# Reordering the hand-over from attention to a GLU block: unit order, an earlier projection, one early weight read, paced reads, later copies and sums

## The chip, the cores and the metric

The kernel runs on one core of one Trainium2 chip. The core has five engines that run their own instruction lists in order and meet only at semaphores: TensorE (PE, with its weight loads PEld), VectorE (DVE), ScalarE (ACT), GpSimd (POOL) and SyncE (SP). SP, ACT and POOL also issue the DMA transfers. The metric is device time in microseconds (us) of one execution; the time before is the median of three runs. The profile is one execution recorded by the hardware profiler; all its times count from the start of its span.

## The reference

The input is x with 2048 rows and 576 columns, in float32. The output is a transformer block:

```python
q, k, v = qkv[0], qkv[1], qkv[2]                 # 32 heads of 18 columns
off = jnp.arange(W) * dil                        # W = 8, dil = 2: rows s, s-2, ..., s-14
idx = pos[:, None] - off[None, :]
...
logits = jnp.einsum("bhsd,bhswd->bhsw", q, kg) * scale
logits = jnp.where(mask[None, None, :, :], logits, -1e9)
attn = _softmax(logits, axis=-1)
o = jnp.einsum("bhsw,bhswd->bhsd", attn, vg)
...
h = x + _A_ref(_layernorm(x, axis=-1), A_wqkv, A_wo)       # attention, projection by wo
g = jnp.einsum("bsd,df->bsf", x, w_gate)                   # F = 4608
u = jnp.einsum("bsd,df->bsf", x, w_up)
h = _sigmoid(g) * u
...
h2 = h + _B_ref(_layernorm(h, axis=-1), B_w_gate, B_w_up, B_w_down)
```

## The kernel before

**Blocks and precision.** The 2048 rows are four blocks of 512: block b stands for even or odd rows (attention looks back in steps of two, so these never mix) and for the first or the second half of them. Every large matrix product is done with operands split into a high and a low part (`split`, line 103: a copy on ACT, a subtraction on DVE) and three matmuls for each pair of parts.

**First stage: QKV, attention, projection of block 0.** `qkv(b, g, ...)` (line 354) is one call: block b, group g of eight heads, four passes of 14 matmuls, one `yield` after each pass, and stores of q, k and v to scratch memory. `attention(at, b, g, o)` (line 159) is one unit for the same pair: it reads q, k and v back on SP and computes the window of eight positions almost entirely on DVE, in 16 steps that end in a `yield`. For block 0 the result stays on the chip in `o`; for the others it is written to scratch by a DMA on POOL (the spill, line 209). `att_all` (line 375) lists the units in the order (0,0), (0,1), (1,0), (1,1), (0,2), (0,3), (1,2), (1,3), and `step(ag, n)` advances that list by n steps between passes of `qkv`. The calls follow their own order; the last ones are (1,2), (0,3), (2,2), (3,2), (1,3), (2,3), (3,3). `front` (line 445) is the projection of block 0: for four tiles of rows it transposes `o`, multiplies by wo, adds x, normalises and transposes again (`proj_j`, line 228), and makes the first GLU operands `X["a00"]` and `X["a01"]`. Lines 471 to 484 set it in place: calls (1,3) and (2,3), then what is missing of unit (0,3), then two rounds of the projection placed behind the last pass, then call (3,3) with one round after each pass, then the rest.

**Second stage: the GLU.** `items` (line 911) is a list of 86 pieces of 128 hidden columns each: 14 "std" for block 0 alone, 22 "pair" for blocks 0 and 1, 14 std for block 1 (operands `X["a10"]` and `X["a11"]`), then 36 pairs for blocks 2 and 3. The variable `c` counts them. An std item is 28 matmuls of 512 columns plus its share of the down projection; a pair item uses seven products in place of eight and runs from operand sums (`s1` to `s4`) of two blocks. The weights of item c + 2 are read into `wg` (`load_gu`, line 502, two buffers) when item c begins, and those of item c + 1 are split (`weights`, line 510). The first two reads go out on POOL (lines 915, 916) into a pool of tiles that is opened when the first stage's pools are closed.

**Work beside the items.** While PE runs items, a second list `bg` is advanced by `bg_step`, eight steps in an std item and up to seven in a pair. `under_first` (line 830) holds what is left of the attention of block 1, then, not before item 5, its projection `proj_scr` (line 751) and the operand sums for the first pairs; `finish_bg` ends it when item 14 begins. `under_rest` (line 847) does the same for blocks 2 and 3. `proj_scr` reads the spilled attention (tiles `oj`), x (tiles `hj`) and the split wo (tile `wow`) through `load_j` (line 745) and line 793 on SP: four `oj` reads with two steps each, then the others during the first two rounds.

**Down projection and the end.** Sums over items are added in DRAM by accumulating DMAs on POOL: `add_dram` (line 667) into `hacc` for blocks 0 and 1, which copies the finished block to the output right after the last addition, and `down_seven` (line 707) into `hsev` for blocks 2 and 3. `seven` (line 996) forms hidden sums in the pool `dk`, which is opened inside item 50 (line 1085) over memory that stage tiles held until then. `load_tails` (line 1016) reads `hsev` back near the end, adds three pieces on DVE at once (line 1029), and waits ten steps; the last down products are added to these tiles and stored.

**The order on each engine** is made when the kernel is built, from the order of the program and its priorities: `tc.high_priority` moves instructions forward among those that are ready, and `tc.issue_after(ins)` keeps the instructions it covers behind `ins` on the same engine's list without any wait of their own.

Of the kernel before, what the change touches and what calls it, by code (L numbers as in the profile page):

```python
# [15 lines left out]
F32 = mybir.dt.float32  # L16
# [44 lines left out]
def kernel(ctx, tc, x, wqkv, wo, wmlp, out):  # L61
# [36 lines left out]
    def f32(ap):  # L98
        return ap.bitcast(F32)
# [274 lines left out]

    def att_all():
        nonlocal o
        for b, g in ((0, 0), (0, 1), (1, 0), (1, 1), (0, 2), (0, 3), (1, 2), (1, 3)):
            while (b, g) not in emitted:
                yield
            if o is None:  # L380
                o = tok_tile()
            yield from attention(at, b, g, None if b else o[:, :, g * CG:(g + 1) * CG])
            if (b, g) == (0, 3):
                for j in range(NS):
                    dve.tensor_copy(o[:, j, D:DX], o[:, j, DM:D])
                ready.append(b)
# [81 lines left out]

    X = {}
    fr = front()  # L470
    for b, g in ((1, 3), (2, 3)):
        for _ in qkv(b, g, T[b], w[g]):
            step(ag, 1 if ready else 4)
    while not ready:
        step(ag, 1)
    last = passes[-1]
    with tc.issue_after(getattr(last, "ins", last)):
        for _ in range(2):
            next(fr)
    for _ in qkv(3, 3, T[3], w[3]):  # L480
        next(fr, END)
        step(ag, 1)
    with tc.high_priority(HI):
        drain(fr)
    ps_stk.close()
# [15 lines left out]

    def load_gu(f, eng=sp, n=WC):
        ws = gw.tile([P, WC], F32, bufs=2, name="wg")
        eng.dma_start(ws[:, :n], wmlp[f][:, :n])
        return ws

    def d_tile():
        return gd.tile([P, 2, D], F32R, bufs=4, name="d")
# [129 lines left out]
        between(6)  # L638

    tails = {}  # L640
    segs = [0] * 2

    def down_tile(seg, t, j):
        js = slice(j * P, (j + 1) * P)
# [21 lines left out]

    def add_dram(b, hs):
        pool.dma_start(hacc[b], hs, accum_op=ALU.add, max_dma_last_dim=8 * D)
        segs[b] += 1
        if segs[b] == 1 + (NF - NSTD) // 2:  # L670
            e, hf = BLOCKS[b]
            pool.dma_start(ov[e, hf], hacc[b])

    def down_units(seg, b):
        hs = st.tile([P, NS, D], F32, name="stage")
# [69 lines left out]
    def load_j(pj, b, j, i):  # L745
        e, hf = BLOCKS[b]
        t = pj.tile([P, D if i else DX], F32, bufs=NS, name="hj" if i else "oj")
        sp.dma_start(t, (xv[e, hf] if i else oscr[b])[:, j])
        return t

    def proj_scr(pj, b, raw, wos, ins=None, after=None):
        e, hf = BLOCKS[b]
        th, tl = th_tile(), tl_tile()

        def tile_j(t, j):
            js = slice(j * P, (j + 1) * P)
            xj = []

            def put(pv, cs):
                if cs.start == 0:  # L760
                    if b < 2:
                        pool.dma_start(hacc[b][:, j], t[1])
                    else:
                        rows = slice(0, 7, 6) if b == 2 else slice(2, 5, 2)
                        pool.dma_start(hsev[:, j // 2, rows, j % 2],
                                       t[1].rearrange("p (i n) -> p i n", i=2))
                    if raw is None:
                        xj.append(pj.tile([P, 5, P], F32, bufs=2, name="xj"))
                act.activation(xj[0][:, cs] if raw is None else raw[:, cs, js], pv, AF.Copy)

            yield from proj_j(bg_bank, t, wos, th[:, :, js], tl[:, :, js], lambda: t[0], put, (1, 0))
            if raw is None:
                act.dma_start(xscr[b][:, :, js], xj[0])

        todo = []
        if ins is None:
            ins = []
            for j in range(NS):
                ins.append([load_j(pj, b, j, 0), None])
                yield  # L780
                yield
            todo = [0, 1, None, 2, 3]
        live = [tile_j(t, j) for j, t in enumerate(ins)]
        n = 0
        for _ in range(5):
            for gn in live:
                if todo and n % 2 == 0:
                    j = todo.pop(0)
                    if j is not None:
                        ins[j][1] = load_j(pj, b, j, 1)  # L790
                    elif wos[0] is None:
                        ww = pj.tile([P, 2, 5, DH2], F32R, name="wow")
                        sp.dma_start(f32(ww), wscr[0])
                        wos[0] = ww[:, 0], ww[:, 1]
                n += 1
                next(gn)
                yield
        nxt = []
        for j, gn in enumerate(live):
            yield from gn  # L800
            if after is not None:
                nxt.append([load_j(pj, after, j, i) for i in range(2)])
        if raw is not None:
            act.dma_start(xscr[b][:, 0:2], raw[:, 0:2])
        return nxt
# [106 lines left out]
             + [("std", 1, f) for f in range(NSTD)] + [("pair", 1, f) for f in range(NF)])  # L912
    bg = under_first()
    with tc.high_priority(2 * HI):
        wg = load_gu(0, pool)
        wg2 = load_gu(1, pool)
        wc = weights("std", wg, True)
    wg = wg2
# [97 lines left out]
    def load_tails():  # L1016
        nonlocal st
        dk_stk.close()
        st_stk.close()
        st = st_stk.enter_context(sb_pool("st3"))  # L1020
        dz = ctx.enter_context(sb_pool("dz", "right"))
        for b, rows in ((2, ((0, 1), (6, None))), (3, ((2, 5), (4, 3)))):
            hs = tails[b] = st.tile([P, 2, 2, 2 * DH2], F32, name=f"tail{b}")
            for h, (k, k2) in enumerate(rows):
                sp.dma_start(hs[:, h], hsev[:, :, k].rearrange("p u i n -> p u (i n)"))
                if k2 is not None:
                    h2 = dz.tile([P, 2, 2 * DH2], F32, name=f"more{b}{h}")
                    sp.dma_start(h2, hsev[:, :, k2].rearrange("p u i n -> p u (i n)"))
                    dve.tensor_tensor(hs[:, h], hs[:, h], h2, ALU.add)
        yield from lag(10)  # L1030

    def twice(i):
        bg_step(i)
# [2 lines left out]

    for c, (kind, p, f) in enumerate(items):
        w, d = wc
        skip = () if kind == "std" else (3,)
        by_seven = c >= NF + NSTD  # L1040
        if c == NSTD:
            finish_bg()
            last_x = splits[-1]
            bg = under_rest(getattr(last_x, "ins", last_x))
        if c == NF + NSTD:
            finish_bg()
            with tc.high_priority(HI):
                for n in ("s1", "a11"):
                    Xn[n] = x_half(*raw[n])
            X = Xn  # L1050
            pp_stk.close()
            dw = ctx.enter_context(sb_pool("dw", "right"))
        if c + 1 < len(items):
            wc = weights(items[c + 1][0], wg, c + 1 < NF + NSTD)
        if c + 2 < len(items):
            wg = load_gu(items[c + 2][2], n=WC if c + 2 < NF + NSTD else GU)
        hid = {}
        blocks = [p] if kind == "std" else [2 * p, 2 * p + 1]

        def last(h0, h1):  # L1060
            hid[0] = hidden(*h0, "h0")
            hid[1] = hidden(*h1, "h1")

        if kind == "std":
            hid = single(X, w, p, late, twice)
        elif not by_seven:
            side = last_pair if c == NF - 1 else bg_step

            def between(i):
                if i in (4, 6):  # L1070
                    units(2)
                side(i)

            pair(X, w, between, last)
        else:
            def between(i):
                nonlocal st, gc, gc_bufs, dk
                units(1)
                if c == NF + NSTD and i == 5:
                    assert not queue  # L1080
                    st_stk.close()
                    gc_stk.close()
                    gc = gc_stk.enter_context(sb_pool("gc2"))
                    st = st_stk.enter_context(sb_pool("st2"))
                    dk = dk_stk.enter_context(sb_pool("dk", "right"))
                    gc_bufs = 2
                down_side(f, i)

            pair(X, w, between, last if f >= NF - NPL else last_sums(f))
            if f < NF - NPL:  # L1090
                if f % 2:
                    if f == 1:
                        queue.append(lag(LAG))
                    queue.append(seven())
                continue
            d = M[f]
        seg.append((hid, d))
        if len(seg) == 2:
            if by_seven and f == NF - NPL + 1:
                queue.append(load_tails())  # L1100
            for b in blocks:
                queue.append(down_std(seg, b, f // 2) if kind == "std" else
                             down_tail(seg, b, f == NF - 1) if by_seven else down_units(seg, b))
            seg = []
# [44 lines left out]
```

## Time and profile before

| | |
|---|---|
| median of 3 runs | 1642.64 us (1641.17 to 1648.43) |
| the profiled execution, its own time | 1647.17 us |
| its span in the profile | 1645.4 us |
| mean granted TensorE clock | 0.979 |
| PE, DVE, ACT, POOL busy | 96%, 78%, 53%, 11% |
| stages of the span, roughly | QKV and attention to 206 us, first items from 251, pairs from 416, second std items from 807, pairs of blocks 2 and 3 from about 1010 to 1616 us, last sums to the end |

The page gives busy shares of every engine and a chain of waits that is followed back from the last instruction. A row of the timeline reads: start, length (both us), engine, line, operation, output and inputs by the program's names, shapes, number of merged instructions, and in brackets how long the engine was idle before it and what ended that time. A row of the chain reads: start, length, what. A row of stretches gives for each engine the busy time and the number of instructions, then the granted clock, the DMA share and GB/s.

### The profile page before, as it was taken

What the parts mean: (1) busy time and instruction counts of PE and PEld (TensorE: products, weight loads), DVE (VectorE), ACT (ScalarE), POOL (GpSimd) and SP (SyncE); (2) the same over time, 40 slices, a digit from 0 to 9 for tenths busy, and PEclk for the clock granted to TensorE, in tenths of its full rate; (3) what the DMA queues carried; (4) which work ended last, traced back from release to release, by engine and by line L of the source; (5) the groups of instructions that cost most, each with busy time, mean ns of one, the idle gap of its engine ahead of it and who ended that gap; (6) DMA issues with size and microseconds to landing.
All of it is one profiled execution on the core that took longest, in us unless ns stands there. A gap on an engine that the chain in (4) does not pass through costs nothing.

```text
span 1645.4 us, 22460 instructions
## 1 busy us (share of the span) xinstructions
PE 1573.6 (96%) x8532; PEld 1392.6 (85%) x8532; DVE 1279.6 (78%) x2002; ACT 873.6 (53%) x1535; POOL 185.2 (11%) x228
## 2 busy tenths in 40 slices
PE   7899887999999999999979999999999999999998
PEld 6799775898888888888968987888888888888887
DVE  7999999558999999999626677777767777677755
ACT  5422224325556566656424344677667776677651
POOL 2000010010000100100111100121121211212210
PEclk9999987999999999999989999999999999999999
DMA  7446635525366666575856335598888888988882
GB/s 252 164 160 230 223 123 186 180 90 190 106 180 154 178 148 175 150 192 142 247 141 215 120 129 147 109 190 174 172 176 163 189 175 172 178 169 177 184 185 91
DMA packets 79613, 276.66 MB, mean 168 GB/s; under 512 B 8368, under 2 KB 16816, under 8 KB 78480
## 3 DMA queue, kind: packets, MB, share of 16 engines
q0 software_dynamic: 28144, 108.74, 34.1%
q1 hardware_dynamic: 40160, 142.75, 27.0%
q10 hardware_dynamic: 11200, 23.73, 3.8%
q8 instruction: 67, 1.10, 0.3%
q14 instruction: 42, 0.34, 0.1%
HBM read 147.19 MB, written 130.35 MB: 169 GB/s over the span
## 4 chain that ended last, share of the span: by engine, by line
PE 62%; issue 15%; DVE 10%; DMA 6%; POOL 4%; ACT 2%; SPq 0%; POOLq 0%; DVEq 0%; ACTq 0%
PE b L544 31%; PE dp L652 14%; PE b L551 6%; PE dp L718 6%; POOL h L727 3%; DMA wg<-in_wmlp_dram 3%; PE acc L150 2%; DVE pr L198 2%; DVE pr L172 1%; DVE lg L175 1%; PE b L150 1%; PE bgp L150 1%; DVE pr L203 1%; DMA h<-stage 1%; DVE pr L205 1%
## 5 line engine op out<-in xcount | busy, mean ns | idle before, releaser
L544 PE MATMUL b<-tl,w 128*128 128x512 f32 x1728 | 447.3, 399 | 18.4 <-DVE w L105 7.6
L544 PEld LDWEIGHTS b<-tl,w 128*128 128x128 f32 x1728 | 315.6, 190 | 80.2 <-DVE w L105 8.3
L544 PE MATMUL b<-th,w 128*128 128x512 f32 x1380 | 359.3, 395 | 0.0
L544 PEld LDWEIGHTS b<-th,w 128*128 128x128 f32 x1380 | 251.9, 189 | 53.7 <-DVE s L626 4.0
L551 PE MATMUL b<-th,w 128*128 128x512 f32 x576 | 178.2, 391 | 0.0
L104 ACT ACTIVATE w<-wg 128x384 fp32r<-128x384 f32 (+2 forms) x200 | 118.1, 596 | 108.7 <-DMA wg<-in_wmlp_dram 45.1
L105 DVE TENSOR_TENSOR w<-wg,w 128x384 fp32r<-128x384 f32 (+2 forms) x200 | 128.5, 648 | 52.6 <-ACT w L104 52.5
L724 ACT ACTIVATE ev<-dp 128x576 f32<-128x576 f32 x224 | 144.8, 647 | 32.9 <-PE dp L718 30.2
L727 POOL DMA_DIRECT2D h<-ev x128 | 109.7, 857 | 461.4 <-ACT ev L724 454.0
L150 PE MATMUL acc<-qw,th 128*128 128x432 f32 x512 | 155.6, 364 | 0.0
L105 DVE TENSOR_TENSOR w<-tw,w 128x512 fp32r<-128x512 f32 x116 | 79.5, 686 | 72.3 <-ACT w L104 71.7
L551 PEld LDWEIGHTS b<-th,w 128*128 128x128 f32 x576 | 108.7, 189 | 23.2
L652 PE MATMUL dp<-d,h0h 128*128 128x288 f32 x640 | 120.6, 298 | 0.0
L652 PE MATMUL dp<-d,h1h 128*128 128x288 f32 x640 | 120.2, 297 | 0.0
L104 ACT ACTIVATE w<-tw 128x512 fp32r<-128x512 f32 x116 | 73.3, 632 | 83.6 <-PE b L544 79.0
L652 PEld LDWEIGHTS dp<-d,h0h 128*128 128x128 f32 x640 | 100.6, 191 | 3.5
L652 PEld LDWEIGHTS dp<-d,h1h 128*128 128x128 f32 x640 | 99.7, 190 | 3.0 <-ACT h1h L104 0.2
L150 PEld LDWEIGHTS acc<-qw,th 128*128 128x128 f32 x512 | 98.1, 192 | 4.8 <-ACT th L104 0.3
L150 PE MATMUL acc<-qw,tl 128*128 128x432 f32 x256 | 93.1, 364 | 0.0
L172 DVE TENSOR_TENSOR pr<-kw,q 128x1152 f32<-128x1152 f32 x64 | 85.3, 1352 | 3.6 <-DMA kw<-k 3.0
L361 ACT ACTIVATE ev<-acc 128x432 f32<-128x432 f32 x64 | 33.3, 527 | 100.9 <-PE acc L153 97.5
L198 DVE TENSOR_TENSOR pr<-vw,lg 128x1152 f32<-128x1152 f32 x64 | 85.2, 1353 | 0.9
(270 smaller groups left out, 2879.6 us busy)
## 6 DMA issues: line engine op xcount, KB each, us to landing
h<-ev POOLq DMA_DIRECT2D x96, 576.0 KB, 6.9
wg<-in_wmlp_dram SPq DMA_DIRECT2D x48, 928.0 KB, 5.4
h<-stage POOLq DMA_DIRECT2D x24, 1152.0 KB, 11.5
wg<-in_wmlp_dram SPq DMA_DIRECT2D x36, 640.0 KB, 4.9
kw<-k SPq DMA_DIRECT2D x16, 792.0 KB, 4.3
vw<-v SPq DMA_DIRECT2D x16, 792.0 KB, 5.7
wd<-in_wmlp_dram SPq DMA_DIRECT2D x18, 576.0 KB, 6.6
h<-ev POOLq DMA_DIRECT2D x32, 288.0 KB, 6.1
```

What stands on the lines that cost most here:

```text
L104: act.activation(hi, src, AF.Copy)
L105: splits.append(dve.tensor_tensor(lo, src, f32(hi), ALU.subtract))
L150: pe.matmul(ps[:, :n], a[:, c, js], m[:, c], start=k == 0, stop=False)
L172: dve.tensor_tensor(pr[:, i], kw[:, j:j + W], q[:, j].unsqueeze(1).broadcast_to([P, W, CG]), ALU.mult)
L198: dve.tensor_tensor(pr[:, i].rearrange("p w (h d) -> p w h d", d=DH), vw[:, j:j + W].rearrange("p w (h d) -> p w h d", d=DH), lg[:, j].uns ...
L361: act.activation(ev[:, :, j], ps[:, :NQ].rearrange("p (t c) -> p t c", t=3), AF.Copy)
L544: pe.matmul(ps, wt[:, a, k0 + c], xx[:, m + c], start=first and k == 0, stop=k == 5, skip_group_check=True)
L551: pe.matmul(ps, wt[:, a, k0], xx[:, 4], start=False, stop=a == 1, skip_group_check=True)
L652: pe.matmul(ps[:, i, :DH2], a[:, js], d[:, m, i * DH2:(i + 1) * DH2], start=k == 0, stop=k == n)
L718: pe.matmul(ps[:, i, :DH2], a[x][:, js], m[y], start=k in (0, 1, 3) and q == 0, stop=q == 2, skip_group_check=True)
L724: act.activation(hs[:, k % 2], ps[:, :, :DH2], AF.Copy)
L727: pool.dma_start(hsev[:, u, k0:k + 1], hs[:, :k + 1 - k0], accum_op=ALU.add, max_dma_last_dim=8 * D)
```

## The change

Six edits. (1) In `att_all`, unit (1,1) goes behind (0,2) and (0,3). (2) The projection of block 0 is placed behind call (1,3); its rounds are then taken between the passes of two calls, (2,3) and (3,3). (3) The weights of the first item are read on SP, after call (2,3) in the program and at high priority, into a slot of the tag `tl` in the pool `xt`, which outlives the first stage; the second item's read stays on POOL. (4) The reads of `proj_scr` are put behind the last weight read on SP, and each behind the one before (`paced`); `oj` reads come three steps apart, `wow` follows them with two steps, and the `hj` reads move by one. (5) The copies of the finished blocks 0 and 1 to the output are issued at items 47 and 55 instead of behind the last addition, and the three sums in `load_tails` come after seven steps, one step each. (6) The pool `dk` hands out three tiles with the names of later ones first, so that they take its first places.

```diff
-        for b, g in ((0, 0), (0, 1), (1, 0), (1, 1), (0, 2), (0, 3), (1, 2), (1, 3)):
+        for b, g in ((0, 0), (0, 1), (1, 0), (0, 2), (0, 3), (1, 1), (1, 2), (1, 3)):
...
-    for b, g in ((1, 3), (2, 3)):
-        for _ in qkv(b, g, T[b], w[g]):
-            step(ag, 1 if ready else 4)
+    for _ in qkv(1, 3, T[1], w[3]):
+        step(ag, 1 if ready else 4)
     while not ready:
         step(ag, 1)
     last = passes[-1]
     with tc.issue_after(getattr(last, "ins", last)):
         for _ in range(2):
             next(fr)
-    for _ in qkv(3, 3, T[3], w[3]):
-        next(fr, END)
-        step(ag, 1)
+    for b in (2, 3):
+        for _ in qkv(b, 3, T[b], w[3]):
+            next(fr, END)
+            step(ag, 1)
+        if b == 2:
+            with tc.high_priority(2 * HI):
+                wg = xt.tile([P, WC], F32, tag="tl", bufs=4, name="wg0")
+                sp.dma_start(wg, wmlp[0])
...
-        eng.dma_start(ws[:, :n], wmlp[f][:, :n])
+        behind[0] = eng.dma_start(ws[:, :n], wmlp[f][:, :n])
         return ws
+
+    behind = [None]
+
+    def paced(dst, src):
+        with tc.issue_after(getattr(behind[0], "ins", behind[0])):
+            behind[0] = sp.dma_start(dst, src)
...
-        segs[b] += 1
-        if segs[b] == 1 + (NF - NSTD) // 2:
-            e, hf = BLOCKS[b]
-            pool.dma_start(ov[e, hf], hacc[b])
...
-        sp.dma_start(t, (xv[e, hf] if i else oscr[b])[:, j])
+        paced(t, (xv[e, hf] if i else oscr[b])[:, j])
...
                 ins.append([load_j(pj, b, j, 0), None])
                 yield
                 yield
-            todo = [0, 1, None, 2, 3]
+                yield
+            ww = pj.tile([P, 2, 5, DH2], F32R, name="wow")
+            paced(f32(ww), wscr[0])
+            wos[0] = ww[:, 0], ww[:, 1]
+            yield
+            yield
+            todo = list(range(NS))
...
-                if todo and n % 2 == 0:
+                if todo and n % 2:
                     j = todo.pop(0)
-                    if j is not None:
-                        ins[j][1] = load_j(pj, b, j, 1)
-                    elif wos[0] is None:
-                        ww = pj.tile([P, 2, 5, DH2], F32R, name="wow")
-                        sp.dma_start(f32(ww), wscr[0])
-                        wos[0] = ww[:, 0], ww[:, 1]
+                    ins[j][1] = load_j(pj, b, j, 1)
...
-        wg = load_gu(0, pool)
         wg2 = load_gu(1, pool)
...
+        adds = []
...
-                    dve.tensor_tensor(hs[:, h], hs[:, h], h2, ALU.add)
-        yield from lag(10)
+                    adds.append((hs[:, h], h2))
+        yield from lag(7)
+        for a, m in adds:
+            dve.tensor_tensor(a, a, m, ALU.add)
+            yield
...
     for c, (kind, p, f) in enumerate(items):
         w, d = wc
+        for b, late_c in ((0, NF + NSTD - 3), (1, NF + NSTD + 5)):
+            if c == late_c:
+                e, hf = BLOCKS[b]
+                pool.dma_start(ov[e, hf], hacc[b])
...
                     dk = dk_stk.enter_context(sb_pool("dk", "right"))
+                    for n in ("s4h", "s4l", "s1h"):
+                        dk.tile([P, TB], F32R, name=n)
```

More of the change, by code (lines that the diff above doesn't have):

```diff
@@ L640 @@
     tails = {}
-    segs = [0] * 2
     def down_tile(seg, t, j):
```

## The prediction

> **What bounds the kernel now.** I read the page first, then the busy times in stretches of 20 us, then TensorE's (PE's) instructions in order of time wherever it stood idle, and last what DVE, SP and POOL did there.
>
> ```profile
> span 1645.4 us, 22460 instructions
> PE 1573.6 (96%) x8532; PEld 1392.6 (85%) x8532; DVE 1279.6 (78%) x2002; ACT 873.6 (53%) x1535; POOL 185.2 (11%) x228
> ```
>
> PE is busy for 1573.6 of 1645.4 us, so 71.8 us of idle time is all that a better order can win, with the slow clock behind each gap. The rows that open the gaps which this change touches (start, length, engine, and in brackets the idle time before and what ended it):
>
> ```profile
> 206.24 0.69 PE L139 MATMUL mm<-ident,tok 128*128 128x128 f32 x2 [7.51 <-DVE tok L206]
> 210.40 0.66 PE L143 MATMUL acc<-ident,tok 128*128 128x128 f32 x2 [3.47 <-DVE tok L385]
> 213.49 0.48 PE L139 MATMUL acc<-ident,tok 128*128 128x128 f32 x1 [2.43 <-DVE tok L206]
> 251.10 1.22 PE L544 MATMUL b<-tl,w 128*128 128x512 f32 x2 [4.78 <-ACT w L104]
> 259.90 2.08 PE L544 MATMUL b<-tl,w 128*128 128x512 f32 x4 [7.58 <-DVE w L105]
> 320.73 1.12 PE L139 MATMUL b<-ident,oj 128*128 128x128 f32 x4 [3.40 <-DVE tl L105]
> 833.44 0.48 PE L143 MATMUL bgp<-ident,oj 128*128 128x128 f32 x1 [8.48 <-DVE tl L105]
> 865.73 0.40 PE L150 MATMUL bgp<-wow,th 128*128 128x288 f32 x1 [3.28 <-DVE hj L243]
> 1021.96 5.53 PE L544 MATMUL b<-tl,w 128*128 128x512 f32 x16 [3.39 <-DVE r L977]
> 1607.42 2.92 PE L544 MATMUL b<-tl,w 128*128 128x512 f32 x6 [2.57 <-ACT s L618]
> ```
>
> These are 46.9 us. Behind each gap the matmuls are slow; the chain of waits shows it beside normal rows of the same shape:
>
> ```profile
> 259.90 4.63 PE b L544 x10
> 268.65 2.72 PE b L544 x12
> 834.57 2.88 PE dp L652 x12
> 872.62 1.58 PE dp L652 x12
> ```
>
> A normal 512-column matmul takes 2.72/12 = 0.227 us, twelve of 288 columns 1.58. So the clock costs another 2.4 us at 260, 1.3 at 834, 1.9 at 1022 (5.53 for 16) and 1.6 at 1607 (2.92 for 6).
>
> **The front (order of attention, projection one call sooner, first weights).** The projection of block 0 waits for unit (0,3) on DVE:
>
> ```profile
> 186.87 2.63 DVE L172 TENSOR_TENSOR pr<-kw,q 128x1152 f32<-128x1152 f32 x2
> 212.97 0.46 DVE L206 TENSOR_TENSOR tok<-pr 128x288 f32<-128x288 f32 x1
> 259.03 1.62 DVE L105 TENSOR_TENSOR w<-wg,w 128x640 fp32r<-128x640 f32 x3
> 100.00:120.00 20.00, 20.00 (x104) 19.14 (x103) 19.03 (x19) 4.03 (x8) 0.00 (x0) 1.00 0.40 144
> ```
>
> The unit spans 26.6 us, some 24 of them attention. Before it DVE has done unit (1,1), which the change puts behind (0,3): the unit would start at 163 and its output be complete at 189. Its data exist then: 104 matmuls in 20 us make a QKV call of 56 last 10.8 us, and four calls lie between (0,3)'s and 197, where PE had finished (2,3) (206.24 less 7.51, less the first transposes), so that (0,3)'s ended at 154; a store and a read of at most 5.4 us each (the weight read below is larger) lead to 165. I take 190 for the output. PE comes to the projection at 186 instead of 197 and waits 4 us instead of 13.4. From 213.5 to 246.3 (251.10 less 4.78) it worked 32.8 us on the projection and one QKV call; with two calls that is 43.6, until 234. The first GLU weights, read on POOL behind the LayerNorms until now, go through SP into a slot that is free after call (1,3), and will have landed; their split on DVE, at 259.03 behind attention steps, can follow the projection. Taken alone, this starts the GLU at 235 and not at 259.9: **25 us**.
>
> DVE takes most of it back. What it must do is not less, only later, and the projection of block 1 needs all of it:
>
> ```profile
> L105 DVE TENSOR_TENSOR w<-wg,w 128x384 fp32r<-128x384 f32 (+2 forms) x15 | 8.6, 597 | 0.5 <-ACT w L104 0.5
> L105 DVE TENSOR_TENSOR d<-wg,d 128x576 fp32r<-128x576 f32 x4 | 3.0, 755 | 0.0
> L564 DVE TENSOR_TENSOR s<-s,b 128x512 f32<-128x512 f32 x4 | 2.7, 687 | 1.8 <-PE b L551 1.8
> L105 DVE TENSOR_TENSOR h0l<-s,h0h 128x512 fp32r<-128x512 f32 x3 | 2.1, 694 | 0.0
> 275.04 0.69 DVE L564 TENSOR_TENSOR s<-s,b 128x512 f32<-128x512 f32 x1 [0.89 <-PE b L551]
> 313.27 0.69 DVE L564 TENSOR_TENSOR s<-s,b 128x512 f32<-128x512 f32 x1 [0.88 <-PE b L551]
> 293.79 0.45 DVE L206 TENSOR_TENSOR kw<-pr 128x288 f32<-128x288 f32 x1
> 302.65 1.75 SPq L748 DMA_DIRECT2D oj<-o  x4
> 398.99 0.69 DVE L109 TENSOR_TENSOR th<-rd,th 64x512 fp32r<-64x512 f32 x1
> 419.07 4.09 PE b L544 x18
> ```
>
> The first four rows are DVE's GLU work from 260 to 294: 16.4 us for 3.5 items, 4.7 an item. Items follow at (313.27 - 275.04)/4 = 9.6 us, so 4.9 us an item are left for attention. At 190 DVE owes three units (72 us), the projection's own work (from 213.4 to 259.0, 45.6 us, it did one unit of 24 and 5 of the next, which leaves 16 to 17) and 3 of first weights; by 235 it has done 45, and 48 of attention remain: 48/4.9 = 9.8 items, 329. The same sum on the old run gives 303 where the last unit ended at 294.2, so it is too long by a fifth of its 43 us: the end lies between 309 and 329, I take 318. After 294.2 came the spill, reads at 302.65, projection and operand sums until 399.7, 105 us, of which some 12 were spent waiting for the projection's place at item 6 (320.73 less 302.65 and a read of 5.4); 318 + 93 = 411. PE needs 235 + 14 x 9.6 + 22 (32.8 less a call) for block 1's projection = 391, so the first pair's run of 18, the first to read the sums, starts at 411 by DVE's chain and not by PE's; it was 419. **8 us** are kept. The bounds: 25 if the list order on PE slides the projection behind later items at no cost; below nothing, the last rival.
>
> What waits behind: a paced read whose spill has not landed stands at the head of SP, and the next weight read stands behind it, one being needed every 9.6 us. The reads' own steps come 6 of 8 steps of an item later, which covers 7 us of this.
>
> **Paced reads, second projection.** In order of time, the SP queue and the chain:
>
> ```profile
> 802.36 2.13 SPq L748 DMA_DIRECT2D oj<-o  x4
> 805.94 0.66 SPq L793 DMA_DIRECT2D wow<-wo  x1
> 811.48 18.86 DMA wg<-in_wmlp_dram
> 861.15 2.03 POOL L867 MEMSET stage<- 128x2304 f32 x1 [10.02 <-DMA h<-stage]
> wg<-in_wmlp_dram SPq DMA_DIRECT2D x48, 928.0 KB, 5.4
> ```
>
> Four oj, two hj and the 1.5 MB of wow were issued ahead of a weight read; it landed after 18.86 us instead of 5.4, ACT stood in its split, and the copies that PE's transposes needed stood behind it: 8.48 + 1.3 us. Paced, the reads come after it, and the first transposes 0.75 item later. I take the whole of it, less 1 for wow meeting a later weight read. The gap at 865.73 comes from POOL: the clearing of a tile waited 10.02 us for an accumulating write, with a LayerNorm's rstd behind it. A projection some 7 us later in the program finds the write landed: 3.28, of which I count 3. Together **12 us**; bounds 3 (reads collide elsewhere) and 17 (with the 3.40 gap at 320.73, not counted since DVE's chain rules there). The Trainium skill, "DMA: Bandwidth & Descriptors", section "Queues, rings and completion order", says that DMA engines go round between the queues packet by packet; POOL's accumulating writes would then still take their turns beside a paced weight read; at half pace it would land after some 11 us (an estimate by that page's rule, twice 5.4), and the term would be 7 and the sum 24.5. The trace cannot tell: no row shows that read without its companions.
>
> **Placeholder tiles.**
>
> ```profile
> 1011.82 1.22 POOL L668 DMA_DIRECT2D h<-stage  x1 [65.19 <-DVE stage L662]
> 1021.21 0.69 DVE L977 TENSOR_TENSOR r<-s,b 128x512 f32<-128x512 f32 x1 [3.56 <-DMA h<-stage]
> ```
>
> The tile of line 977 shares memory with a stage tile and had to wait until that one's write landed, with PE's bank behind it; three tiles that are needed two items later take this place, and the new one lies over tiles that are done. The gap and its clock go, 3.39 + 1.9: **5.3 us**, bounds 0 and 5.3.
>
> **Tail sums.**
>
> ```profile
> 1604.26 1.36 DVE L1029 TENSOR_TENSOR tail<-tail,more 128x1152 f32<-128x1152 f32 x1 [2.90 <-DMA tail<-h]
> 1616.79 23.97 PE dp L652 x180
> DMA to landing us min/median/max: 2.2/2.5/6.5
> ```
>
> DVE stood 2.90 us before its first sum with PE's evacuation behind it. Seven steps later (a pair of 17 us has seven) the reads are long in. The three sums, 4.1 us, then fall into the last 24 us, where DVE does 16 additions of 0.75: 12 us, so there is room. The gap and its clock go, 2.57 + 1.6: **4.2 us**, bounds 0 and 5. The Trainium skill, "TensorE: Matmul & The Clock Gate", section "What's actually happening", gives an idle window of about 3.4 us before the clock is halved; by it this gap would cost 2.6 and the sum would be 1.6 less. The trace differs: six matmuls took 2.92 us behind a gap of 2.57.
>
> **Output copies.** Two issues of 0.7 us move to items 47 and 55, the second among the seven-product pairs; any write to the output landed within 6.5 us (last row above), and nobody waits for these. 0, bounds -3 and 2.
>
> **Sum.** 8 + 12 + 5.3 + 4.2 = 29.5 us. The profiled execution took 1647.17 (1.8 outside its span) and would take 1617.7; it lies 4.5 above the median 1642.64, from which I get **1613.0** (rounded).
>
> **Rivals.**
> - DVE is the bound outright: PE meets the projection of block 1 at item 6.75, near 300, and stands until about 328; nothing of the front is kept. With 7.25 items and 22 us to go that is 420, as before. For: DVE's sum above. Against: the last unit ended 26 us before the transposes at 320.73 that wait for it, so the chain has slack. 1621.
> - The order gives way on PE: 25 kept at the front. 1596.
> - The reads and writes collide somewhere else: 3 for the second projection instead of 12. 1622.
> - The change does not do what it says: PE's order still puts the projection's transposes ahead of free QKV work as at 206, and pacing only swaps who is late; only placeholders and tails win, 9.5. 1633.
> - **Slower:** the weight and hidden splits, of higher priority, starve attention on DVE. If only 3.4 us an item are left, the 48 us last all 14 items, to 369; then 93 us of chain run with no GLU item over them, the first pair starts near 460, 43 later than now, against 21.5 won elsewhere: 1664. It decides when unit (1,3) ends later than about 347; against it, the old run's sum erred to the other side.
>
> **How the numbers follow.** Forecast 0.47; DVE outright 0.17; order gives way 0.13; collision 0.11; not as said 0.06; slower 0.06. Range 1595 to 1632, leaving out the last two and some edges. 0.5% is 8.2 us, about what a measurement can tell from no change: faster 0.85, same 0.09, slower 0.06.
>
> **What would show it.** First GLU matmul near 235, unit (1,3) ending near 318, the first pair's run of 18 near 411; no PE gap over 3 us near 825, 1010 and 1575; wg landing under 10 us at the second projection. Wrong if that run starts after 419, or if a weight read on SP is found standing behind an oj read.

## The result and the profile after

The changed kernel took 1618.55 us (median of 4 runs, 1617.61 to 1624.51) beside 1645.54 for the kernel before in the same comparison: a ratio of 0.9844, 95% interval 0.9805 to 0.9883. That is 27.0 us less; 29.5 were forecast, to 1613.0. The spans of the two profiled executions differ by 28.6 us. The head of the changed kernel's page:

```profile
span 1616.8 us, 22443 instructions
PE 1570.3 (97%) x8532; PEld 1387.0 (86%) x8532; DVE 1277.2 (79%) x2002; ACT 877.2 (54%) x1537; POOL 184.8 (11%) x227
```

PE does the same 8532 matmuls and its idle time fell from 71.8 us to 46.5. The rows of its timeline in the changed kernel that answer to those of before (columns as there):

```profile
191.41 1.12 PE L139 MATMUL acc<-ident,tok 128*128 128x128 f32 x4 [2.12 <-DVE tok L206]
239.12 1.45 PE L554 MATMUL b<-tl,w 128*128 128x512 f32 x4 [2.24 <-ACT w L104]
242.07 2.08 PE L554 MATMUL b<-tl,w 128*128 128x512 f32 x4 [1.49 <-DVE w L105]
327.74 1.12 PE L139 MATMUL b<-ident,oj 128*128 128x128 f32 x4 [2.96 <-DMA oj<-o]
401.79 2.55 PE L554 MATMUL b<-th,w 128*128 128x512 f32 x6 [2.26 <-DVE s L574]
936.37 0.53 PE L661 MATMUL dp<-d,h1h 128*128 128x288 f32 x2 [2.42 <-ACT h1h L104]
1579.99 2.92 PE L554 MATMUL b<-tl,w 128*128 128x512 f32 x6 [4.09 <-ACT s L628]
```

The 7.51 and 3.47 before the projection of block 0 and the 4.78 and 7.58 before the first items have shrunk to waits of 1.0 to 2.2; the 8.48 and 3.28 at the second projection and the 3.39 before the seven-product pairs are gone. Two things went the other way: the gap before the tail grew from 2.57 to 4.09, and the wait of 2.42 at 936, with one of 1.01 just behind it, is new.

To see where the 28.6 us were won I follow landmarks, events that can be found in the other kernels too: the first GLU items (end of the last wait for their weights), the first pair's run of 18 matmuls, the first and the last sigmoid of the second set of 14 std items (between them lies the second projection), line 977's first product (line 982 after) and the last run of 180 matmuls. These rows give them, of before:

```profile
803.92 0.60 ACT L588 ACTIVATE s<-b 128x512 f32<-128x512 f32 x1 [1.68 <-PE b L551]
993.48 0.60 ACT L588 ACTIVATE s<-b 128x512 f32<-128x512 f32 x1 [3.22 <-PE b L551]
```

and of after, from ACT's and DVE's timelines and the chain of waits:

```profile
790.38 0.60 ACT L598 ACTIVATE s<-b 128x512 f32<-128x512 f32 x1 [1.74 <-PE b L561]
969.03 0.60 ACT L598 ACTIVATE s<-b 128x512 f32<-128x512 f32 x1 [2.08 <-PE b L561]
```

```profile
993.28 0.68 DVE L982 TENSOR_TENSOR r<-s,b 128x512 f32<-128x512 f32 x1
```

```profile
405.20 4.37 PE b L554 x18
1588.31 23.97 PE dp L661 x180
```

| stretch | before | after | won |
|---|---|---|---|
| start to the first items | 259.90 | 242.07 | 17.8 |
| to the first pair's run of 18 | 159.2 | 163.1 | -4.0 |
| to the first std sigmoid | 384.9 | 385.2 | -0.3 |
| to the last of them (second projection) | 189.6 | 178.7 | 10.9 |
| to line 977's first product | 27.7 | 24.2 | 3.5 |
| to the last run of 180 | 595.6 | 595.0 | 0.6 |
| to the end of the span | 28.6 | 28.5 | 0.1 |

The front keeps 13.9 us, the second projection gives 10.9, and all that follows it, where the placeholder tiles and the tail sums were to win 9.5, gives 4.1.

A landmark comes from one profiled execution. Three profiles of what is the same program (this one, its repetition and the kernel without edit 5, both below) have the first pair at 405.2, 405.6 and 402.2, so some 3 us at the front say nothing. Behind it the stretches repeat better: 177.9 to 178.7 us between the two sigmoids, 618.5 to 619.3 from the second of them to the last run of 180.

### The profile page after: what moved, and what is told of

Its sections match the earlier page's. It is cut to its first block, busy times and chain, and to the rows that moved or that the text cites. A ratio compares the mean times of both kernels' runs of the same rounds, so it can differ in the third digit from the quotient of the medians.

```text
span 1616.8 us, 22443 instructions
## 1 busy us (share of the span) xinstructions
PE 1570.3 (97%) x8532; PEld 1387.0 (86%) x8532; DVE 1277.2 (79%) x2002; ACT 877.2 (54%) x1537; POOL 184.8 (11%) x227
## 4 chain that ended last, share of the span: by engine, by line
PE 64%; issue 17%; DVE 8%; DMA 6%; POOL 4%; ACT 1%; SPq 0%; POOLq 0%; ACTq 0%; DVEq 0%
PE b L554 30%; PE dp L661 13%; PE acc L150 6%; PE dp L723 6%; PE b L561 5%; POOL h L732 3%; DMA wg<-in_wmlp_dram 2%; DVE lg L175 1%; DVE w L105 1%; DVE pr L172 1%; DVE pr L198 1%; PE bgp L150 1%; PE b L150 1%; DMA o<-kw 1%; DMA kw<-k 1%
## 5 line engine op out<-in xcount | busy, mean ns | idle before, releaser
L561 PE MATMUL b<-th,w 128*128 128x512 f32 x576 | 178.0, 391 | 0.0
L669 ACT ACTIVATE stage<-dp 128x576 f32<-128x576 f32 x96 | 62.2, 648 | 53.3 <-PE dp L661 42.4
## 6 DMA issues: line engine op xcount, KB each, us to landing
h<-stage POOLq DMA_DIRECT2D x24, 1152.0 KB, 11.7
```

Source lines behind the costliest of these rows:

```text
L561: pe.matmul(ps, wt[:, a, k0], xx[:, 4], start=False, stop=a == 1, skip_group_check=True)
L669: act.activation(hv, ps, AF.Copy)
```

## The experiments

The kernels ran in three comparisons, each beside the kernel before on its own chip (1645.26, 1643.59 and 1646.38 us). At first I held, as the prediction did, that the second projection needs the paced reads. The runs led to another theory: the front's gain is the order of attention, and the second projection's is the place of the reads on SP, however it comes about.

**Edits 1 to 3 alone** (order, projection, early weights; no pacing, no placeholders, old copies and sums).

> The kernel before with edits 1 to 3 alone (unit order, projection behind call (1,3), first weights on SP in their own slot). Landmarks: the first pair's run of 18 (419.07 before, 405.20 after the change), the last sigmoid of the second std items (993.48 and 969.03). Theory: the front earns its 14 us by itself and nothing else changes: the run of 18 near 405, the last sigmoid near 980, the time near 0.9915 of before (1631). Rival: the first projection also needs the paced reads, since the oj reads would again hold up a weight read: run of 18 at 411 or later, time 0.995 or more (1638).

It took 1618.98 us, 0.9843 (0.9821 to 0.9865): as fast as the full change and 12 us faster than I had expected. The first pair stood at 401.6, near the expected 405; the last sigmoid stood at 967.4 and not near 980, because the 8.48 us gap was gone without any pacing. SP and ACT in this kernel show why:

```profile
771.86 2.04 SPq L752 DMA_DIRECT2D oj<-o  x4
785.44 0.42 SPq L797 DMA_DIRECT2D wow<-wo  x1
794.08 0.33 SPq L508 DMA_DIRECT2D wg<-in_wmlp_dram  x1
```

```profile
805.09 0.74 ACT L104 ACTIVATE w<-wg 128x640 fp32r<-128x640 f32 x1 [3.77 <-DMA wg<-in_wmlp_dram]
```

The four `oj` reads happen to stand one weight read earlier on SP than before, so only `wow` and `hj` still travel with the next weights, which land after 11.0 us instead of 18.86. Between the sigmoids lie 180.8 us. The wait behind POOL that was 3.28 us before is still there:

```profile
838.85 0.61 PE L150 MATMUL bgp<-wow,th 128*128 128x288 f32 x1 [3.81 <-DVE hj L243]
```

So is the wait that the placeholder tiles were to remove:

```profile
994.72 0.69 DVE L980 TENSOR_TENSOR r<-s,b 128x512 f32<-128x512 f32 x1 [3.15 <-DMA h<-stage]
```

**The full change without the rule that paces, its later steps kept.**

```diff
-        paced(t, (xv[e, hf] if i else oscr[b])[:, j])
+        sp.dma_start(t, (xv[e, hf] if i else oscr[b])[:, j])
...
-            paced(f32(ww), wscr[0])
+            sp.dma_start(f32(ww), wscr[0])
```

> The changed kernel with the later steps of the projection reads kept, but the reads issued freely on SP instead of behind the last weight read. Theory: the issue order on SP is what ended the gap of 8.48 us at the second projection (a weight read that lands after 18.86 us); without it the weight read is late again and the time goes back by 8 to 11 us, to 1628. Rival: the later place of the projection alone does it, so that a late weight read meets no transposes: time as after the change, within 3 us of 1618.6.

1620.38 us, 0.9846 (0.9831 to 0.986), the same span as the full change (1616.8) and 178.0 us between the sigmoids. My theory of 1628 failed and its rival held: the rule itself was not needed.

**Tail sums kept behind the last item's hidden products on DVE.** Shown are the lines that place the sums; the list `mults` that collects the hidden products, and the old place of the sums, which goes, are left out.

```diff
...
+            if f == NF - 1:
+                with tc.issue_after(getattr(mults[-1], "ins", mults[-1])):
+                    for a, m in adds:
+                        dve.tensor_tensor(a, a, m, ALU.add)
...
```

> The changed kernel with the three sums over the tails kept behind the last item's two hidden products on DVE's list. Theory: emitting them seven steps later left them at the same place of DVE's list, ahead of the sums of the last item, so that DVE still waits there for the tail reads; behind the products they cost nothing, the gap of 4.09 us and 1.6 us of slow clock go: 1613, ratio to the changed kernel 0.9965. Rival: the last item is held by the tail reads in any case, through the first additions of down products into these tiles: time unchanged, the gap moves by one row.

1613.72 us, 0.981 (0.9793 to 0.9827). In PE's timeline the gap of 4.09 is gone and another has come nearer the end:

```profile
1585.15 0.53 PE L663 MATMUL dp<-d,h0h 128*128 128x288 f32 x2 [2.61 <-DVE tail L673]
```

From the last std sigmoid to the end of the span lie 645.0 us, against 646.9 to 647.8 in the five profiles that have the sums ahead of the evacuation and are otherwise alike: some 2 us. The medians don't show it. The next kernel, which turned out to be the full change under other line numbers, took 1614.51 us in the same comparison, and 0.8 us lie well inside the intervals.

**The full change without edit 5** (copies and sums where they were).

> The changed kernel with edit 5 undone (output copies behind the last addition, tail sums at once and ten steps of wait). Theory: every engine's list has the same instructions in the same order as the changed kernel's, so it is the same program but for line numbers: 1618.6 within the noise, with the gap near 1580 unchanged. Rival: the later emission does change what waits: 1 to 4 us slower, as the tail gap of before was priced.

1614.51 us, 0.9809 (0.9791 to 0.9826). The theory held: the built instruction lists of all five engines are, instruction for instruction, those of the full change. So edit 5 cannot have an effect, and 1614.51 beside 1618.55 is how far two comparisons of one program can differ. The changed kernel's DVE shows what the edit meant to change:

```profile
1576.84 1.36 DVE L1038 TENSOR_TENSOR tail<-tail,more 128x1152 f32<-128x1152 f32 x1 [4.43 <-DMA tail<-h]
1578.11 0.68 DVE L623 TENSOR_TENSOR s<-s,b 128x512 f32<-128x512 f32 x1
1579.91 2.63 DVE L1038 TENSOR_TENSOR tail<-tail,more 128x1152 f32<-128x1152 f32 x2 [1.12 <-DMA tail<-h]
```

The first sum still stands ahead of the instruction that empties PE's result bank (line 623, the evacuation) and now waits 4.43 us for its read. Moving the sums to a later line of the program did not move them in the built list; `issue_after`, in the experiment before, did.

**Edit 4 alone on the old kernel.**

> The kernel before with edit 4 alone (paced and later projection reads). Prediction's theory: it takes away the gap of 8.48 us at the second projection and the one of 3.28 us behind it, 12 us: 1633, ratio 0.993. The rival after the run with edits 1 to 3 alone, which had no such gap without any pacing: the gap comes from how late DVE's attention of blocks 2 and 3 ends against PE's items, and pacing only changes who meets whom: gain under 6 us, ratio 0.997 or more.

1628.73 us, 0.9915 (0.989 to 0.994), span 1623.9. The 12 us came: between the sigmoids lie 177.9 us instead of 189.6, 11.7 won. The first pair came 5.9 earlier (413.2), and the gap of 3.40 at block 1's transposes, which the prediction had left out of this term, is gone there as well.

**Edit 1 alone: the order of attention.**

> The kernel before with edit 1 alone: units (0,2) and (0,3) ahead of (1,1), the projection still behind call (2,3), the first weights still on POOL. Theory: the output of block 0 is complete at 190, before PE ends call (2,3) at 197, so all 13.4 us of waiting go without any second call to fill it; GLU from about 246 since the weight read still waits behind the LayerNorms: 1628, ratio 0.989. Rival: PE's list or the weight read eats it, under 6 us: 1640.

1635.82 us, 0.9947 (0.9924 to 0.997), span 1628.1: 7.8 us won by the medians, about half of what I had expected. The profiled execution took 1629.9, 5.9 below the median of its kernel, so its landmarks flatter it. PE at the first items and at the second projection:

```profile
242.07 1.65 PE L544 MATMUL b<-tl,w 128*128 128x512 f32 x3 [10.83 <-ACT w L104]
247.74 2.08 PE L544 MATMUL b<-tl,w 128*128 128x512 f32 x4 [4.02 <-DVE w L105]
819.42 0.48 PE L143 MATMUL bgp<-ident,oj 128*128 128x128 f32 x1 [7.96 <-DVE tl L105]
```

The first pair's run of 18 starts at 405.6, where the full change has 405.2. In this execution the one line is enough for all that the front keeps; the medians leave room for less, and how much it is in a usual execution is not shown. At the second projection next to nothing is won: 188.4 us, with the reads and the landing as before. SP's rows and the chain's:

```profile
788.87 2.03 SPq L748 DMA_DIRECT2D oj<-o  x4
792.43 0.49 SPq L793 DMA_DIRECT2D wow<-wo  x1
797.99 0.33 SPq L504 DMA_DIRECT2D wg<-in_wmlp_dram  x1
```

```profile
797.99 18.34 DMA wg<-in_wmlp_dram
```

**Edits 1 and 2** (first weights still on POOL).

> Edits 1 and 2 without 3: as the run with edits 1 to 3 but with the first weights read on POOL. Theory: the weight read on POOL comes behind the LayerNorms at about 220 and lands before PE is through the second call at 237, so the slot of its own is worth little: within 3 us of 1619. Rival: it lands after 240 or its memory comes free late, and the GLU starts 5 us or more later: 1624 or more.

1631.01 us, 0.9921 (0.9899 to 0.9943), span 1630.0. I had expected it within 3 us of 1619; that was wrong. The profile shows the missing 12 us where I did not look for them: the first pair stands at 405.4, 3.8 behind edits 1 to 3 (little more than the spread of one program), and the gap at the second projection is back:

```profile
246.49 2.07 PE L544 MATMUL b<-tl,w 128*128 128x512 f32 x4 [1.25 <-DVE w L105]
820.36 0.48 PE L143 MATMUL bgp<-ident,oj 128*128 128x128 f32 x1 [9.06 <-DVE tl L105]
```

So the early weights bring the first items 4 us forward (246.49 to 242.47), and the other 10 us (190.9 between the sigmoids, 180.8 with edit 3) come from the `oj` reads, which stand on the other side of a weight read in the two built lists. Nothing in edit 3 asks for that, so I took it for a side effect of building the lists anew. Two experiments followed to test it.

**Edit 4's later steps on the old kernel, without the rule** (edit 4 alone, with the two lines of the second experiment undone).

> The old kernel with the later steps of the projection's reads (oj three steps apart, wow ahead of the hj reads, hj a step later) but without the rule that holds them behind the last weight read; the lists of PE, POOL and, but for one pair of neighbours, DVE are those of pace_only. Theory (the later steps alone let the oj and wow reads pass between two weight reads): the wait of 8.48 near 833 is gone, the first to the last std sigmoid of the second set takes 177 to 180 us as in pace_only (177.9), time 1626 to 1632. Rival (the rule itself does it, as the prediction argued): a weight read still lands after 15 us or more, a PE gap of 5 us or more near 800 to 835, 186 us or more between the two sigmoids, time 1636 to 1644.

1632.97 us, 0.9933 (0.9908 to 0.9958), span 1629.6, and 178.8 us between the sigmoids. The theory held, with a time 1 us above its range. SP's queue and ACT:

```profile
785.77 1.49 SPq L754 DMA_DIRECT2D oj<-o  x3
799.20 0.43 SPq L754 DMA_DIRECT2D oj<-o  x1
800.49 0.32 SPq L790 DMA_DIRECT2D wow<-wo  x1
808.32 0.33 SPq L504 DMA_DIRECT2D wg<-in_wmlp_dram  x1
```

```profile
820.08 0.74 ACT L104 ACTIVATE w<-wg 128x640 fp32r<-128x640 f32 x1 [5.97 <-DMA wg<-in_wmlp_dram]
```

Three of the `oj` reads went 22.5 us ahead of the weight read, which landed after 11.74 us; PE's gap was 1.11.

**The full change with the first weights on POOL** (edit 3 undone).

> The full change with the first GLU weights read on POOL as before (edit 3 undone). Theory (what edit 3 won in front_only against order_place, 12 us, was the place of the second projection's reads against the weight reads, which edit 4 sets here anyway): first pair's run of 18 at 404 to 408, 177 to 181 us from the first to the last std sigmoid of the second set, time within 4 us of the changed kernel. Rival (the early weights are worth it by themselves, by an earlier first GLU item): run of 18 at 410 or later, 7 to 12 us above the changed kernel.

1616.11 us, 0.9821 (0.9806 to 0.9837), beside 1619.12, 0.9839 (0.9824 to 0.9853), of the full change in the same comparison; the run of 18 at 405.8 and 179.4 us between the sigmoids. With the reads' place set by edit 4, edit 3 is worth nothing that shows, as the theory had it; that the first items start 4 us later there (246.4 against 242.1) no longer shows at the first pair.

**A better version?** Edits 1 to 3 and 6, no pacing, tail sums held back as above.

> Edits 1 to 3 and 6, no pacing, output copies as before, and the three tail sums kept behind the last item's hidden products. Theory: the front's 26 us, 3.5 of the placeholder tiles, 5 of the tail sums, and none of the two waits of 2.4 and 1.0 us that the paced kernel shows near 936: 1645.3 - 35 = 1610, ratio 0.979. Rival: the terms do not add, since what comes earlier waits for the same transfers later: 1614 or more, as the changed kernel with the tail sums fixed.

1613.39 us, 0.9831 (0.9806 to 0.9856): 30.2 us won where I had expected 35. It was then run beside the full change:

> The changed kernel once more, for a comparison in one call with best_again: 1614 to 1620, PE gap of 3.5 to 4.3 near 1576 to 1580. If the earlier 4 us between it and the same program without edit 5 were the chip's, it comes out anywhere in this range.

> Edits 1 to 3 and 6 with the tail sums held behind the last hidden products, no pacing. Theory (the tail sums' wait of 3 to 4 us and the paced weight reads near 385 to 402 are real costs of the change): 3 to 7 us faster than after_again in this call. Rival (the difference lay between calls): within 2 us of it.

It took 1615.72 us, 0.9814 (0.9792 to 0.9836), the full change 1619.12. The medians differ by 3.4 us, which my theory allowed, but the intervals overlap, so whether it is faster stays open. Its own two profiles differ by 6.0 us of span, 4 of which are there at the first pair (400.1 and 404.0).

## Why the prediction came out right

**What bounds.** PE's idle time and its slow clock were the right thing to count: the 28.6 us are 25.3 of idle time less and the clock behind it.

**The front: kept 13.9 us, forecast 8.** The output of block 0 was complete at 191.4 (forecast 190) and unit (1,3) ended at 318.8 (forecast 318):

```profile
190.89 0.46 DVE L206 TENSOR_TENSOR tok<-pr 128x288 f32<-128x288 f32 x1
318.34 0.45 DVE L206 TENSOR_TENSOR kw<-pr 128x288 f32<-128x288 f32 x1
387.47 0.69 DVE L109 TENSOR_TENSOR th<-rd,th 64x512 fp32r<-64x512 f32 x1
```

The items started at 242, not 235: PE arrived at 236.9 and then waited 2.24 and 1.49 us for the splits of the weights, which I had counted as ready. The step that failed is "411 by DVE's chain and not by PE's". The operand sums ended at 388.2, 69 us behind the unit's end and not 93: the old chain of 105 us had slack in it, since PE held it up. Stretches of the kernel before had shown that, from the transposes to the sums:

```profile
330.00:350.00 20.00, 20.00 (x133) 18.81 (x132) 9.37 (x22) 3.40 (x9) 1.11 (x2) 1.00 0.18 63
390.00:410.00 20.00, 20.00 (x115) 17.84 (x114) 17.18 (x27) 8.26 (x16) 0.00 (x0) 1.00 0.48 174
```

PE (the first busy time of a row) worked all 20 us of each, and DVE (the third) only 9.37 in the first. PE's own sum was the right one: 242.1 + 156.4 (14 items of 9.6 and 22 for the projection) + 6.2 of gaps is 404.7, measured 405.2. It fits the kernel before as well: 259.9 + 156.4 + 3.4 is 419.7, measured 419.07. So the first pair had been PE's before the change too, and in every other kernel here the same sum, from its own first items and its gaps over 0.8 us, comes within 3.6 us of the first pair. The rival that PE's order keeps all of the front came nearest in kind: 17.8 were won at the first items, and 4.0 lost again to small gaps (2.96, 0.99 and 2.26) and their clock, against 3.40 before.

**Second projection: 10.9 us, forecast 12.** The term had two parts. For the larger, 9.8 us less 1, the mechanism is shown (a weight read that shares the queue with the reads), and so is its size. What failed is the inference that the reads must be paced to end it. Seven kernels put the landing of that weight read beside the wait of PE behind it:

| kernel | weight read lands after | PE's gap |
|---|---|---|
| before | 18.9 | 8.48 |
| edit 1 | 18.3 | 7.96 |
| edits 1, 2 | 19.4 | 9.06 |
| edit 4's steps alone | 11.7 | 1.11 |
| full change, not paced | 11.3 | 0.66 |
| edits 1 to 3 | 11.0 | none over 0.8 |
| full change | 6.5 | none over 0.8 |

Up to 11.7 us cost PE next to nothing here; 18 and more cost it 8 to 9. Each of the orders that put three or four of the `oj` reads one weight read apart from `wow` was enough. So edits 1 to 3 and edit 4 remove the same wait (8.8 and 11.7 us won between the sigmoids), and their gains don't add: the spans fell by 29.9 and 21.5 alone, by 28.6 together with the rest.

The smaller part, 3 us for the wait of 3.28 behind POOL's accumulating write, came true and was lost again. With edit 4's later steps that wait is gone (0.86 us at most); with edits 1 to 3 and without those steps it is 3.60 to 3.81 in three profiles. But all eight profiles with the later steps, and none of the six others, have a new wait of PE of 1.9 to 2.4 us between 933 and 947, and one of 1.0 behind it. In the changed kernel DVE stands there for the read of `ar`, which POOL issues when the projected x is written, and the hidden product that PE needs stands behind it on DVE's list:

```profile
933.83 1.23 DVE L262 TENSOR_TENSOR rs<-ar 128x1024 f32<-128x1024 f32 x1 [3.92 <-DMA ar<-x]
```

Counted back from the last std sigmoid, that read goes out 41.3 us ahead of it, and 47.5 in the kernel before, where DVE waits 0.46 for it. That the later steps are what moved it rests on which kernels have the wait; a kernel with the later steps and an earlier `ar` was not run.

The weight read of the changed kernel landed after 6.5 us, though three `oj` reads stand ahead of it on SP, the last sign of being wrong that the prediction named; they were issued 9 us earlier (788.76):

```profile
797.88 0.33 SPq L508 DMA_DIRECT2D wg<-in_wmlp_dram  x1
```

```profile
804.39 0.74 ACT L104 ACTIVATE w<-wg 128x640 fp32r<-128x640 f32 x1 [0.71 <-DMA wg<-in_wmlp_dram]
```

By the Trainium skill, "DMA: Bandwidth & Descriptors", section "Queues, rings and completion order" (the engines go round between queues packet by packet), I had estimated 11 us beside POOL's writes and a term of 7. Accumulating writes of POOL went out at 788.37 and 800.83, on either side of this read, and take 11.7 us to land in the median; so the row speaks against that estimate of mine for this place. The term wouldn't have shrunk either way, since a landing after 11 us costs PE next to nothing.

**Placeholders: forecast 5.3, measured 0 to 4.8.** The wait of line 977 is gone and 3.5 us with it: from the last std sigmoid to that product lie 24.1 to 24.2 us in all eight profiles with the tiles, 27.1 to 27.7 in all six without. But from the last std sigmoid to the last run of 180 the kernel before took 623.3 us and the changed one 619.3, and the five others without placeholders and with the old tail sums took 619.2 to 621.7; the four others with the placeholders and the tail sums in the same place (full change again, not paced, without edit 5, without edit 3) took 618.5 to 618.9. Measured so, the tiles are worth 0 to 4.8 us; the means of the two sets are 2.0 apart. (No two kernels differ by edit 6 alone.) The clock term was over-sized: the 16 matmuls behind the wait took 5.53 us in the one profile of before, but 4.06 to 4.08 in four of the five others, so that little was to be won there. And some of it comes back as a longer wait at the tail: PE's gap there is 3.65 to 4.27 us in the kernels with placeholders and 2.57 to 3.06 in those without. The row of edits 1 to 3 alone shows the difference:

```profile
1576.66 1.36 DVE L1032 TENSOR_TENSOR tail<-tail,more 128x1152 f32<-128x1152 f32 x1 [3.10 <-DMA tail<-h]
```

Counted from the last std sigmoid, DVE comes to this sum 606.2 us later there and 603.4 in the changed kernel, and the read ends the wait after 609.3 and 607.8: the work is 2.8 us sooner there, the read only 1.5.

**Tail sums: forecast 4.2, measured 0.** The step that failed is "seven steps later the reads are long in": the sums were not issued later at all, and the gap that they were to remove stood at 4.09. The chain of the changed kernel shows that the read itself is late, behind an accumulating write:

```profile
1563.47 7.43 DMA h<-ev
...
1571.05 5.67 DMA tail<-h
...
1576.84 0.10 DVE tail L1038
...
1579.99 2.92 PE b L554 x6
```

Tied behind the hidden products the sums remove the gap, and 2.61 us come back at the last hidden products' down matmuls, which wait behind 3.89 us of sums on DVE: the "room" of the prediction was there, but not at that moment.

**Output copies: 0.** As forecast, though for a simpler reason: they were issued at the same place as before.

So the sum of 29.5 was right within 1 us of span by luck, because its errors met: the front was 5.9 too small, placeholders and tail together 5.4 and the projection 1.1 too large. What stays open: whether edits 1, 4 (or its steps alone) and 6 would give it all. By the landmarks they should; it wasn't tried. Nor was any order that avoids both the wait behind POOL and the one for `ar`.

## What to carry to other kernels

Before you charge a moved piece of work to the engine that runs it, ask in that very stretch which engine is never idle, and try its sum on the old kernel first: here PE's sum met the landmark within 1 us before any edit, and DVE's chain, which ended near it, had slack. When two edits remove the same wait, run each alone, and compare landmarks rather than totals, since a rebuilt instruction list can move a queue's order elsewhere and win or lose 10 us that the edit has no claim to. Look for new waits as well as for those that are gone. To delay an instruction, tie it to another one; moving its line in the program may leave the built list as it was.

## What the runs showed of the hardware

A 928 KB weight read took 5.4 us in the median, 11.0 to 11.7 with the 1.5 MB of `wow` and one or a few of the smaller reads issued shortly before it on SP, and 18.3 to 19.4 with four `oj` reads as well: three kernels of each kind agree within 1.1 us. By an estimate, 2 to 3 us of the step from 11 to 18 are not the `oj` reads' own: the weight read is issued 5.5 to 5.7 us behind `wow` in the three slow cases and 7.8 to 8.6 in the three others, so `wow` had that much longer to pass.

The matmul clock drops behind gaps shorter than I had assumed. The four matmuls at 242.07 took 2.08 us, behind gaps of 2.24 and 1.49 with 1.45 us of work between them; four of the same shape 4 us later took half of it:

```profile
246.40 1.07 PE L554 MATMUL b<-tl,w 128*128 128x512 f32 x4
```

The granted clock is 1.00 from 239.0 to 240.6 and 0.50 from 242.0 to 244.2; the stretch around them comes to 0.88 (after the length come the busy times of PE, PEld, DVE, ACT and POOL, then the clock, the DMA share and GB/s):

```profile
236.00:250.00 14.00, 10.27 (x37) 7.53 (x36) 12.39 (x13) 6.18 (x10) 0.00 (x0) 0.88 0.99 389
```

The Trainium skill, "TensorE: Matmul & The Clock Gate", section "What's actually happening", says that the clock is halved after at least one idle window of about 3.4 us; neither gap is so long, and the trace shows the halved rate all the same.
